# Weight loading of a convolution and feed-forward kernel: the first matrix in four transfers, the second in two buffers shared with the output

## The chip, the cores and the metric

The kernel runs on one core of one Trainium2 chip. The metric is the device time of one execution in microseconds (us). A run that differs by less than 0.2%, some 2.3 us here, is counted as the same.

## The reference

Two stages follow each other. The first is a causal convolution over seven positions whose weights are made for each token and each of eight heads by a softmax; the second is a feed-forward layer of width 2048.

```python
w = exp(weight_gen - max(weight_gen)); w = w / (sum(w) + 1e-09)      # (4, 4096, 8, 7)
x = einsum('bshk,bskhg->bshg', w, x_unf)      # 7 rows of x, ending at the token; 192 columns
h = x.reshape(16384, 192) @ w_in              # 192 x 2048
g = where(h >= 1, h, where(h <= -1, 0, (h + 1) ** 2 / 4))
out = (g @ w_out).astype(float32)             # 2048 x 192
```

The matrices `w_in` and `w_out` arrive as 64-bit floating point numbers, 3.15 MB each; the kernel turns them into 32-bit ones itself.

## The kernel before

The 16384 tokens are worked through in 32 blocks of 512. For one block the 2048 columns of `w_in` are 16 pieces of 128, taken two at a time: eight "pairs" for a block, 256 in all. Each pair has a first product (`gemm1_pair`, 18 matmuls), an activation on ScalarE and VectorE (`relu`, `square`, `act_g`, `split_g`), and a second product (`gemm2_part`, twice 16 matmuls), which is issued two pairs later. The convolution of later blocks runs on GpSimd beside this. All instructions stand on their engine in the order in which the code is written, so an instruction that waits holds up everything behind it on its engine.

The weights are decoded once, in the pairs of the first block, in eight chunks; chunk c is what pair c needs: 192 x 256 numbers of `w_in` ("part 0") and 256 x 192 of `w_out` ("part 1"). For each part `cast_act` (ScalarE) or `cast_dve` (VectorE) makes the upper bits in a buffer `head`, of which there are two; `merge` (VectorE) shifts the lower bits in and writes `psw` in PSUM; `high` (ScalarE) and `low` (VectorE) split the result in two summands, `whi` and `wlo` for part 0, `wo` for part 1. `marks` holds the VectorE steps so that GpSimd's part of the convolution of block 1 (`wave`) goes behind them.

`load_weights(c)` fills a buffer `r` from a pool of four with three transfers on SyncE's queue (SP): one for each half of the partitions from `w_in`, one for 128 partitions from `w_out`. A row of `w_in` in such a transfer has 128 numbers, 1024 bytes. Chunks 0, 1 and 2 are issued first, then the tokens of block 1 (`load_x(1)`), then chunk 3. Chunks 4 to 7 are issued when the buffer of the chunk four places before is free. The first transfer is held back until a step of the softmax of block 0 (`marks[6]`). The store of a finished block goes through a tile `osb` from a pool of two. A transfer also waits for the one issued eight places before it on the same queue.

In the code that sets the beginning in order, the steps stand so:

```python
add(3)
cast_act(0, 0)
again(own[0])
...                       # the transposes of block 0 follow, on TensorE
merge(0, 0)
cast_dve(0, 1)
...
cast_dve(1, 2)            # both parts of chunk 1 in one instruction
merge(1, 0)
```

`again` copies 64 columns of a tile of the convolution, so that the transposes (`turn_sum`, line 267) of block 0 can read it; they wait for the last of these copies.

Of the kernel before, what the change touches and what calls it, by code (L numbers as in the profile page):

```python
# [22 lines left out]
def kernel(  # L23
# [22 lines left out]
    P = 128  # L46
    B, S, D = x.shape
# [6 lines left out]
    Q = P // 2  # L54
    NC = D // Q
# [20 lines left out]
    raw = ctx.enter_context(tc.tile_pool(name="raw", bufs=4))  # L76
# [7 lines left out]
    op = ctx.enter_context(tc.tile_pool(name="op", bufs=2))  # L84
# [10 lines left out]
    heads = [const.tile([P, (D // Q) * P + 2 * D, 2], U16, tag=f"head{m}", name="head") for m in range(2)]  # L95
# [4 lines left out]
    def run(ops):  # L100
        for o in ops:
            o()
# [194 lines left out]
    CF = 2  # L297
    C1 = NC * P
    CN = C1 + CF * D
    NCH = NF // CF  # L300
    UNIT = 2.0 ** 8
    raw_t, marks = {}, []

    def load_weights(c, behind=None):
        r = raw.tile([P, 4 * CN + 2], U16, tag="r", name="r")
        for h in range(2):
            f = c * CF + h
            load = nc.sync.dma_start(
                out=r[h * Q:(h + 1) * Q, 1:1 + 4 * C1].rearrange("q (k c) -> q k c", k=NC),
                in_=w_in[:, f * P:(f + 1) * P].rearrange("(k q) c -> q k c", q=Q).bitcast(U16))  # L310
            if behind is not None:
                tc.add_manual_dep(load.ins, behind.ins.name, SYNC, reason="the first block goes first")
                behind = None
        nc.sync.dma_start(
            out=r[:, 1 + 4 * C1:1 + 4 * CN].rearrange("p (f c) -> p f c", f=CF),
            in_=w_out[c * CF * P:(c + 1) * CF * P, :].rearrange("(f p) c -> p f c", p=P).bitcast(U16))
        raw_t[c] = r

    def tops(c, part):

        sl = (slice(0, C1), slice(C1, CN), slice(0, CN))[part]
        top = raw_t[c][:, 2:2 + 4 * CN].rearrange("p (c t) -> p c t", t=4)[:, sl, 2]
        return heads[c % 2][:, sl, 1].bitcast(F16), top.bitcast(BF16)

    def cast_act(c, part):
        o, i = tops(c, part)
# [2 lines left out]
    def cast_dve(c, part):  # L329
        o, i = tops(c, part)  # L330
        marks.append(nc.vector.tensor_scalar(out=o, in0=i, scalar1=0.5, scalar2=None, op0=ALU.mult))  # L331

    psw = {}

    def merge(c, part):
        word = raw_t[c].bitcast(U32)[:, 1:1 + 2 * CN].rearrange("p (c t) -> p c t", t=2)[:, :, 0]
        upper = heads[c % 2].rearrange("p c t -> p (c t)").bitcast(U32)
        psw[c, part] = ps_h.tile([P, 512], F32, tag="h", name="psw")
        sl = (slice(0, C1), slice(C1, CN))[part]
        marks.append(nc.vector.scalar_tensor_tensor(  # L340
            out=psw[c, part].bitcast(U32)[:, 0:sl.stop - sl.start], in0=word[:, sl], scalar=13, in1=upper[:, sl],
            op0=ALU.logical_shift_right, op1=ALU.bitwise_or))

    def views(c, part):
# [5 lines left out]
    def high(c, part):  # L350
        hi, lo, src = views(c, part)
        nc.scalar.activation(out=hi, in_=src, func=AF.Copy)
# [95 lines left out]
    def evac(b):  # L448

        t0 = b * N  # L450
        osb = op.tile([P, 4, D], F32, tag="osb", name="osb")
        pos = o_t.pop(b)
        by_turn = osb.rearrange("p (k m) d -> p m k d", m=n // 2)
        ops = []
        for m in range(n // 2):
            ops.append(lambda m=m: nc.scalar.activation(out=by_turn[:, m], in_=pos[m][:, :, D:2 * D], func=AF.Copy, scale=UNIT ** 2))  # L456
            ops.append(lambda m=m: nc.vector.scalar_tensor_tensor(  # L457
                out=by_turn[:, m], in0=pos[m][:, :, 0:D], scalar=UNIT ** 2, in1=by_turn[:, m],
                op0=ALU.mult, op1=ALU.add))

        def store(m=None):
            rows = out[t0:t0 + N, :]
            if b < 2:
                nc.sync.dma_start(out=rows.rearrange("(p j) d -> p (j d)", j=n), in_=osb.rearrange("p j d -> p (j d)"))
            elif m is None:
                nc.sync.dma_start(out=rows.rearrange("(a q) d -> q a d", q=P), in_=osb)
            else:
                nc.sync.dma_start(out=rows.rearrange("(k m q) d -> q m k d", q=P, m=n // 2)[:, m], in_=by_turn[:, m])

        return ops, store  # L470
# [60 lines left out]
    with tc.manual_schedule():  # L531
# [10 lines left out]
        clear_x(1)  # L542
        s0, s1 = softmax(0), softmax(1, nc.gpsimd, nc.gpsimd)
        marks += [o() for o in s0[0:3] + s1[0:2] + s0[3:]]
        load_weights(0, marks[6])
        load_weights(1)
        load_weights(2)
        load_x(1)
        load_weights(3)
        run(s1[2:4])  # L550
        alone, near, far, second, add, own = conv_summed(0)
        src = [ps_h.tile([P, 512], F32, tag="h", name="psx") for _ in range(NC)]
# [16 lines left out]
        run(s1[4:6])  # L569
        low(0, 0)  # L570
        run(split_x(0, src, [nc.vector] * NC))
        cast_dve(1, 2)
        merge(1, 0)
        turned1 = whole()
        n_ops = conv(1, nc.gpsimd, marks, turned1)
# [10 lines left out]

        def first_pairs():
            merge(0, 1)
            merge(1, 1)
            tc.add_manual_dep(s1[6]().ins, marks[-1].ins.name, SYNC, reason="the decoding of a chunk goes first")  # L590
            load_weights(4)
            load_weights(5)
            relu(0)
            high(1, 0)
            low(1, 0)
            gemm1_pair(1)
            cast_act(2, 0)
            high(0, 1)
            high(1, 1)
            low(0, 1)  # L600
            low(1, 1)
            cast_dve(2, 1)
            merge(2, 0)
            merge(2, 1)
            wave(3)
            load_weights(6)
            square(0)
            relu(1)
            high(2, 0)
            high(2, 1)  # L610
            square(1)
            act_g(0)
            low(2, 0)
            low(2, 1)
            act_g(1)
            split_g(0)
            relu(2)
            square(2)
            split_g(1)
            relu(3)  # L620
            square(3)
            act_g(2)
            act_g(3)
            split_g(2)
            split_g(3)
            cast_act(3, 0)
            cast_dve(3, 1)

        def early_pair(w):
            i, j, c = 2 * w, 2 * w + 1, w + 1  # L630
            merge(c, 0)
            merge(c, 1)
            wave(1)
            if c + 4 < NCH:
                load_weights(c + 4)
            relu(i)
            high(c, 0)
            high(c, 1)
            low(c, 0)
            low(c, 1)  # L640
            square(i)
            relu(j)
            square(j)
            act_g(i)
            if c + 1 < NCH:
# [28 lines left out]
        for w in range(NS // 2 + LAGP):  # L674
            i, j = 2 * w, 2 * w + 1
# [74 lines left out]
```

## Time and profile before

| | |
|---|---|
| runs | 1160.45, 1161.01, 1163.01 us; median 1161.01 |
| profiled execution, first to last instruction (span) | 1158.6 us, 2.4 us under the median of the runs |
| TensorE busy | 1145.0 us, 99% of the span |
| VectorE, ScalarE, GpSimd busy | 72%, 83%, 68% |
| moved by DMA | 91.43 MB, 79 GB/s in the mean |

The span is the time inside the program; the difference to the runs lies around it. TensorE is PE in the rows, its weight loads PEld; VectorE is DVE, ScalarE is ACT, GpSimd is POOL, SyncE's queue is SPq. A time in a row counts from the start of the span. "Busy" of TensorE includes time in which a matmul waits inside the engine, so 99% alone does not say that it does useful work at its peak.

### The profile page before, as it was taken

The page shows a single profiled execution, that of the slowest core. Times are in us where ns is not written, and L with a number is a line of the kernel's source. Part 1 is how long each engine was busy: PE and PEld are TensorE (multiplying, and loading weights), DVE is VectorE, ACT ScalarE, POOL GpSimd, SP SyncE. Part 2 cuts the span into 40 slices and gives each one's busy share as a digit, 9 for nine tenths or more (in the row PEclk, how much of TensorE's full clock was granted, in tenths as well). Part 3 has the DMA queues.
Part 4 walks back from the last instruction along what each step waited for, and adds up shares of the span by engine and source line. Part 5 has one row for each costly group of instructions (what it writes and reads, how often), then busy time and mean ns, then how long its engine had stood idle before and what let it go on. Part 6 is the DMA issues. An engine that isn't in the chain of part 4 may idle for free.

```text
span 1158.6 us, 32197 instructions
## 1 busy us (share of the span) xinstructions
PE 1145.0 (99%) x12885; PEld 1038.1 (90%) x12885; DVE 834.1 (72%) x1271; ACT 964.7 (83%) x1745; POOL 792.5 (68%) x511
## 2 busy tenths in 40 slices
PE   7999999999999999999999999999999999999998
PEld 5799999999999999999999999999999999999997
DVE  8887767677676776767777676776767767677664
ACT  6878888888888888888888888888888888888886
POOL 4788976667857678486686866678576785866310
PEclk9999999999999999999999999999999999999999
DMA  9422222212222212222121222222222122221100
GB/s 229 112 82 79 77 84 90 89 64 73 75 77 90 84 61 82 71 87 90 56 89 59 85 89 90 64 73 74 76 90 95 51 85 70 80 90 57 47 24 15
DMA packets 84052, 91.43 MB, mean 79 GB/s; under 512 B 5056, under 2 KB 75712, under 8 KB 83904
## 3 DMA queue, kind: packets, MB, share of 16 engines
q1 hardware_dynamic: 83904, 89.39, 24.0%
q8 instruction: 101, 1.65, 0.6%
q14 instruction: 47, 0.39, 0.1%
HBM read 64.99 MB, written 24.38 MB: 77 GB/s over the span
## 4 chain that ended last, share of the span: by engine, by line
PE 95%; ACT 2%; DMA 2%; DVE 1%; issue 0%; POOL 0%; DVEq 0%; POOLq 0%; ACTq 0%; SPq 0%
PE o L432 48%; PE psh L378 45%; DMA r<-in_moe_w_in_dram 1%; PE psx L267 1%; DMA r<-in_moe_w_out_dram 1%; PE psx L208 0%; ACT u L392 0%; DVE psh L397 0%; ACT u L389 0%; ACT gh L403 0%; DVE psw L340 0%; DVE gl L404 0%; POOL piece L189 0%; POOL acc L189 0%; ACT hc L258 0%
## 5 line engine op out<-in xcount | busy, mean ns | idle before, releaser
L432 PE MATMUL o<-wo,gh 64*128 64x384 f32 x4096 | 612.2, 355 | 1.5 <-SPq L441 1.4
L397 DVE SCALAR_TENSOR_TENSOR psh<-u,psh 128x512 f32<-128x512 f32 x512 | 354.7, 696 | 299.6 <-ACT u L392 299.4
L432 PE MATMUL o<-wo,gl 64*128 64x192 f32 x4096 | 542.7, 251 | 0.0
L432 PEld LDWEIGHTS o<-wo,gh 64*128 64x128 f32 x4096 | 421.1, 184 | 13.1 <-SPq L441 2.3
L432 PEld LDWEIGHTS o<-wo,gl 64*128 64x128 f32 x4096 | 421.3, 187 | 9.0
L389 ACT ACTIVATE u<-psh 128x512 f32<-128x512 f32 x512 | 301.5, 589 | 93.2 <-PE psh L378 91.2
L404 DVE TENSOR_TENSOR gl<-psh,gh 128x512 fp32r<-128x512 f32 x512 | 345.7, 686 | 15.3 <-ACT gh L403 1.1
L403 ACT ACTIVATE gh<-psh 128x512 fp32r<-128x512 f32 x512 | 299.2, 592 | 65.5 <-DVE psh L397 65.5
L378 PE MATMUL psh<-hc,whi 64*128 64x512 f32 x1536 | 349.8, 404 | 3.7 <-DVE wlo L356 1.9
L189 POOL TENSOR_TENSOR acc<-acc,pr 128x768 f32<-128x768 f32 x185 | 343.8, 1858 | 5.7 <-DVE head L331 2.0
L378 PE MATMUL psh<-hl,whi 64*128 64x512 f32 x1536 | 337.7, 391 | 0.0
L378 PE MATMUL psh<-hc,wlo 64*128 64x512 f32 x1536 | 337.3, 390 | 0.0
L392 ACT ACTIVATE u<-u 128x512 f32<-128x512 f32 x512 | 323.7, 632 | 16.0
L179 POOL TENSOR_TENSOR pr<-x,w 128x768 f32<-128x768 f32 x186 | 286.8, 1549 | 7.1 <-DVE psw L340 7.1
L259 POOL TENSOR_TENSOR hl<-XT,hc 128x512 fp32r<-128x512 f32 x90 | 115.4, 1297 | 221.2 <-ACT hc L258 221.2
L378 PEld LDWEIGHTS psh<-hl,whi 64*128 64x128 f32 x1536 | 173.6, 185 | 34.7 <-DVE hl L259 0.3
L378 PEld LDWEIGHTS psh<-hc,whi 64*128 64x128 f32 x1536 | 173.0, 185 | 29.4 <-DVE wlo L356 4.3
L378 PEld LDWEIGHTS psh<-hc,wlo 64*128 64x128 f32 x1536 | 174.1, 187 | 21.4
L179 POOL TENSOR_TENSOR acc<-x,w 128x768 f32<-128x768 f32 x31 | 47.9, 1547 | 72.5 <-DVE w L155 70.6
L258 ACT ACTIVATE hc<-XT 128x512 fp32r<-128x512 f32 x90 | 55.5, 618 | 0.0
L284 DVE STREAM_TRANSPOSE T<-acc 128x768 f32<-128x768 f32 x30 | 50.9, 1698 | 0.3 <-POOL acc L189 0.3
L457 DVE SCALAR_TENSOR_TENSOR osb<-o,osb 128x384 f32<-128x384 f32 x64 | 32.7, 556 | 2.7 <-ACT osb L456 2.7
(44 smaller groups left out, 188.8 us busy)
## 6 DMA issues: line engine op xcount, KB each, us to landing
x<-in_x_dram SPq DMA_DIRECT2D x28, 960.0 KB
XT<-D SPq DMA_DIRECT2D x180, 128.0 KB
out_dram<-osb SPq DMA_DIRECT2D x31, 384.0 KB
D<-T SPq DMA_DIRECT2D x30, 384.0 KB
x<-in_x_dram SPq DMA_DIRECT2D x4, 945.0 KB
w<-in_weight_gen_dram SPq DMA_DIRECT2D x15, 224.0 KB
r<-in_moe_w_in_dram SPq DMA_DIRECT2D x16, 192.0 KB
r<-in_moe_w_out_dram SPq DMA_DIRECT2D x8, 384.0 KB
```

Of the source, the lines that this page charges most:

```text
L179: held(eng.tensor_tensor(out=t, in0=xtile[:, k:k + n, :].rearrange("p j (h g) -> p j h g", h=H), in1=wt[:, gi, :, :, k:k + 1].to_broadcast ...
L189: held(eng.tensor_tensor(out=o, in0=s, in1=t, op=ALU.add))
L258: ops.append(lambda c=c: nc.scalar.activation(out=hc[:, c], in_=src[c], func=AF.Copy))
L259: ops.append(lambda c=c: lows.append(engines[c].tensor_tensor(out=hl[:, c], in0=src[c], in1=hc[:, c].bitcast(F32), op=ALU.subtract)))
L284: lambda: nc.vector.transpose(out=T.rearrange("p b c j -> p b j c"), in_=acc.rearrange("p j (r b) -> p b j r", b=R)),
L378: nc.tensor.matmul(out=pair[h][:, 0:N], lhsT=l[rows, f // 2, (c + h) % NC if b < 2 else c], rhs=r[rows, c], start=(s == 0), stop=(s == len ...
L389: nc.scalar.activation(out=u_t[i], in_=h_t[i][:, 0:N], func=AF.Relu, scale=0.5 * UNIT, bias=0.5)
L392: nc.scalar.activation(out=u_t[i], in_=u_t[i], func=AF.Square, scale=UNIT ** -0.5)
L397: nc.vector.scalar_tensor_tensor(out=pv, in0=uv, scalar=1.0 / UNIT, in1=pv, op0=ALU.min, op1=ALU.max)
L403: nc.scalar.activation(out=gh[:, 0:N], in_=gv, func=AF.Copy)
L404: nc.vector.tensor_tensor(out=gl[:, 0:N], in0=gv, in1=gh[:, 0:N].bitcast(F32), op=ALU.subtract)
L432: mm = nc.tensor.matmul(out=o_t[b][turn][:, k, 0:cols], lhsT=g_t[i][l][rows, t * P:(t + 1) * P], rhs=wo[rows, f].rearrange("p s d -> p (s ...
```

## The change

`w_in` is loaded by `load_in` for four chunks at once: two calls, each with two transfers (one for each half of the partitions), 192 rows of 512 numbers, 4096 bytes, each. So that these columns are neighbours, chunk c now has the columns c and 8 + c (in pieces of 128) instead of 2c and 2c + 1, and `load_out` takes the rows of `w_out` to match. `load_out(c)` still loads 256 rows of `w_out`, 1536 bytes to a row, in one transfer over 128 partitions, but into one of the two tiles `osb`, which the stores use later. `cast_dve(1, 2)` becomes two instructions, and `cast` and `merge` read part 0 in three pieces of 128 columns.

```diff
-    def load_weights(c, behind=None):
-        r = raw.tile([P, 4 * CN + 2], U16, tag="r", name="r")
+    def load_in(c, behind=None):
+        r = raw.tile([P, 4 * WIDE * C1 + 2], U16, tag="ri", name="ri", bufs=2)
         for h in range(2):
-            f = c * CF + h
+            at = (h * NCH + c) * P
             load = nc.sync.dma_start(
-                out=r[h * Q:(h + 1) * Q, 1:1 + 4 * C1].rearrange("q (k c) -> q k c", k=NC),
-                in_=w_in[:, f * P:(f + 1) * P].rearrange("(k q) c -> q k c", q=Q).bitcast(U16))
+                out=r[h * Q:(h + 1) * Q, 1:1 + 4 * WIDE * C1].rearrange("q (k c) -> q k c", k=NC),
+                in_=w_in[:, at:at + WIDE * P].rearrange("(k q) c -> q k c", q=Q).bitcast(U16))
...
+    def load_out(c):
+        r = op.tile([P, 4 * CF * D + 2], U16, tag="osb", name="ro")
         nc.sync.dma_start(
-            out=r[:, 1 + 4 * C1:1 + 4 * CN].rearrange("p (f c) -> p f c", f=CF),
-            in_=w_out[c * CF * P:(c + 1) * CF * P, :].rearrange("(f p) c -> p f c", p=P).bitcast(U16))
-        raw_t[c] = r
+            out=r[:, 1:1 + 4 * CF * D].rearrange("p (f c) -> p f c", f=CF),
+            in_=w_out.rearrange("(h s p) c -> s p h c", h=2, p=P)[c].bitcast(U16))
+        out_t[c] = r
...
-        load_weights(0, marks[6])
-        load_weights(1)
-        load_weights(2)
+        load_in(0, marks[6])
+        load_out(0)
+        load_out(1)
         load_x(1)
-        load_weights(3)
+        load_in(4)
...
-        cast_dve(1, 2)
+        cast_dve(1, 0)
+        cast_dve(1, 1)
         merge(1, 0)
...
             merge(0, 1)
             merge(1, 1)
...
-            load_weights(4)
-            load_weights(5)
+            load_out(2)
+            load_out(3)
...
-            load_weights(6)
+            load_out(4)
...
-            if c + 4 < NCH:
-                load_weights(c + 4)
+            if c + 2 < NCH:
+                load_out(c + 2)
```

Two places show how the order on the engines changes. The first is SyncE's queue at the beginning, from the first weight transfer on; `r` is the buffer of a chunk, `DMAHW` with a number is a wait for an earlier transfer, `DVE`, `PE` and `Activation` are waits for those engines. Before:

```order
L308 DMA r<-in_moe_w_in_dram 64x3x512 [waits DVE_49]
L308 DMA r<-in_moe_w_in_dram 64x3x512
L314 DMA r<-in_moe_w_out_dram 128x2x768
L308 DMA r<-in_moe_w_in_dram 64x3x512 [waits DMAHW0_49]
L308 DMA r<-in_moe_w_in_dram 64x3x512 [waits DMAHW1_49]
L314 DMA r<-in_moe_w_out_dram 128x2x768 [waits DMAHW2_49]
L308 DMA r<-in_moe_w_in_dram 64x3x512 [waits DMAHW3_49]
L308 DMA r<-in_moe_w_in_dram 64x3x512 [waits DMAHW4_49]
L314 DMA r<-in_moe_w_out_dram 128x2x768 [waits DMAHW5_49]
L126 DMA x<-in_x_dram 128x1920 [waits DMAHW6_49]
```

And the same place of the change, where `ri` is the buffer of `w_in` for four chunks and `ro` that of `w_out` for one:

```order
L309 DMA ri<-in_moe_w_in_dram 64x3x2048 [waits DVE_49]
L309 DMA ri<-in_moe_w_in_dram 64x3x2048
L320 DMA ro<-in_moe_w_out_dram 128x2x768
L320 DMA ro<-in_moe_w_out_dram 128x2x768 [waits DMAHW0_49]
L126 DMA x<-in_x_dram 128x1920 [waits DMAHW1_49]
L309 DMA ri<-in_moe_w_in_dram 64x3x2048 [waits DMAHW2_49]
L309 DMA ri<-in_moe_w_in_dram 64x3x2048 [waits DMAHW3_49]
L320 DMA ro<-in_moe_w_out_dram 128x2x768 [waits DMAHW7_49,DMAHW4_49,DVE_49]
L320 DMA ro<-in_moe_w_out_dram 128x2x768 [waits DMAHW5_49,DMAHW0_49,DVE_49]
```

The transfer of `w_out` for chunk 2 stood ahead of the tokens of block 1; now it stands behind them and behind both transfers of `w_in` for chunks 4 to 7, and it waits for VectorE besides.

The second place is VectorE, from the cast of chunk 1 to the activation of the first pair (`psw`, `whi`, `wlo`, `wo` and `head` as above). Before:

```order
L331 TENSOR_SCALAR head<-r 128x768 [waits DMAHW2_49,DMAHW1_49,DMAHW0_49]
L340 SCALAR_TENSOR_TENSOR psw<-r,head 128x384 [waits DVE_49]
L340 SCALAR_TENSOR_TENSOR psw<-r,head 128x384 x2
L356 TENSOR_TENSOR wlo<-psw,whi 128x384 [waits Activation_49]
L356 TENSOR_TENSOR wo<-psw,wo 128x2x192 [waits Activation_49] x2
L331 TENSOR_SCALAR head<-r 128x384 [waits DMAHW5_49]
L340 SCALAR_TENSOR_TENSOR psw<-r,head 128x384 [waits DMAHW4_49,DMAHW3_49,DVE_49]
```

And of the change:

```order
L347 TENSOR_SCALAR head<-ri 128x384
L347 TENSOR_SCALAR head<-ro 128x384 [waits DMAHW0_49]
L356 SCALAR_TENSOR_TENSOR psw<-ri,head 128x384 [waits DVE_49]
L356 SCALAR_TENSOR_TENSOR psw<-ro,head 128x384
L356 SCALAR_TENSOR_TENSOR psw<-ro,head 128x384 [waits DVE_49]
L373 TENSOR_TENSOR wlo<-psw,whi 128x384 [waits Activation_49]
L373 TENSOR_TENSOR wo<-psw,wo 128x2x192 [waits Activation_49] x2
L347 TENSOR_SCALAR head<-ro 128x384 [waits DMAHW4_49,DVE_49]
```

The order of the steps is the same but for the cast that became two. The last row is the cast of chunk 2's `w_out`; the transfer that it waits for is the one that the second merge in these rows lets go.

## Rows read from the trace of the kernel before

**Rows 1.** Page, part 1: busy time, share of the span, instructions.

```profile
PE 1145.0 (99%) x12885; PEld 1038.1 (90%) x12885; DVE 834.1 (72%) x1271; ACT 964.7 (83%) x1745; POOL 792.5 (68%) x511
```

**Rows 2.** Chain that ended last, 0 to 110 us: start, length, what.

```profile
20.21 11.32 DMA r<-in_moe_w_in_dram
...
31.55 6.98 DMA r<-in_moe_w_out_dram
...
56.86 0.66 PE psx L267 x4
...
58.84 2.12 PE psh L378 x18
60.95 2.27 PE o L432 x32
```

**Rows 3.** Busy time by stretch: stretch, length, engines, PEclk, DMA share, GB/s.

```profile
24.00:30.00 6.00, 4.09 (x44) 3.39 (x42) 5.36 (x11) 5.21 (x11) 2.94 (x3) 1.00 1.10 199
...
sum 42.00, PE 36.77 PEld 29.10 DVE 39.14 ACT 35.38 POOL 22.93; mean PE 5.25 PEld 4.16 DVE 5.59 ACT 5.05 POOL 3.27
```

**Rows 4.** Waits of the engines, 0 to 60 us: all that name a DMA.

```profile
POOL piece L227 <- DMA x<-in_x_dram: 1.2, 1, 1.2
...
DVE m L149 <- DMA w<-in_weight_gen_dram: 0.8, 2, 0.4
```

**Rows 5.** Timeline of ACT and POOL: start, length, what, [idle before <- releaser].

```profile
6.92 4.54 POOL L227 TENSOR_TENSOR piece<-x,w 128x768 f32<-128x768 f32 x3 [1.18 <-DMA x<-in_x_dram]
...
11.81 0.63 ACT L327 ACTIVATE head<-r 128x384 f16<-128x384 bf16 x1
12.64 0.42 ACT L169 ACTIVATE piece<-piece 128x256 f32<-128x256 f32 x1 [0.19 <-DVE piece L244]
```

**Rows 6.** Timeline of DVE, 12 to 39 us.

```profile
12.99 0.38 DVE L331 TENSOR_SCALAR head<-r 128x384 f16<-128x384 bf16 x1
...
16.46 0.61 DVE L331 TENSOR_SCALAR head<-r 128x768 f16<-128x768 bf16 x1
17.10 1.50 DVE L340 SCALAR_TENSOR_TENSOR psw<-r,head 128x384 uint32<-128x384 uint32 x3
...
20.14 0.39 DVE L331 TENSOR_SCALAR head<-r 128x384 f16<-128x384 bf16 x1
...
24.64 0.69 DVE L404 TENSOR_TENSOR gl<-psh,gh 128x512 fp32r<-128x512 f32 x1 [0.48 <-ACT gh L403]
...
28.07 1.03 DVE L340 SCALAR_TENSOR_TENSOR psw<-r,head 128x384 uint32<-128x384 uint32 x2
...
36.01 0.39 DVE L331 TENSOR_SCALAR head<-r 128x384 f16<-128x384 bf16 x1
...
37.16 1.45 DVE L404 TENSOR_TENSOR gl<-psh,gh 128x512 fp32r<-128x512 f32 x2
```

**Rows 7.** Timeline of SyncE's queue: when transfers are issued.

```profile
5.80 1.36 SPq L308 DMA_DIRECT2D r<-in_moe_w_in_dram  x2
...
11.75 0.47 SPq L126 DMA_DIRECT2D x<-in_x_dram  x1
```

**Rows 8.** DMA view, 0 to 8 us: GB/s in 40 slices of 0.2 us.

```profile
GB/s 0 0 0 0 0 0 0 0 22 148 246 215 224 237 305 502 234 86 499 307 307 499 230 384 384 307 307 461 346 269 85 0 0 0 0 0 51 138 236 318
```

**Rows 9.** DMA views of 11:12, 27:28, 13:14 and 17:19.5 us, in this order.

```profile
DMA packets 181, 0.17 MB, mean 173 GB/s; under 512 B 12, under 2 KB 181, under 8 KB 181
...
DMA packets 191, 0.18 MB, mean 184 GB/s; under 512 B 15, under 2 KB 191, under 8 KB 191
...
DMA packets 210, 0.30 MB, mean 296 GB/s; under 512 B 8, under 2 KB 210, under 8 KB 210
...
DMA packets 223, 1.06 MB, mean 422 GB/s; under 512 B 16, under 2 KB 103, under 8 KB 223
```

**Rows 10.** Timeline of PE, 19 to 29 us: pair 1's end, pair 2's start.

```profile
20.86 0.61 PE L378 MATMUL psh<-hl,whi 64*128 64x512 f32 x2
22.56 0.96 PE L378 MATMUL psh<-hc,whi 64*128 64x512 f32 x2 [1.08 <-DVE wlo L356]
```

More of the change, by code (lines that the diff above doesn't have):

```diff
@@ L301 @@
     UNIT = 2.0 ** 8
-    raw_t, marks = {}, []
-    def load_weights(c, behind=None):
-        r = raw.tile([P, 4 * CN + 2], U16, tag="r", name="r")
+    WIDE = 4
+    in_t, out_t, marks = {}, {}, []
+    def load_in(c, behind=None):
+        r = raw.tile([P, 4 * WIDE * C1 + 2], U16, tag="ri", name="ri", bufs=2)
         for h in range(2):
-            f = c * CF + h
+            at = (h * NCH + c) * P
             load = nc.sync.dma_start(
-                out=r[h * Q:(h + 1) * Q, 1:1 + 4 * C1].rearrange("q (k c) -> q k c", k=NC),
-                in_=w_in[:, f * P:(f + 1) * P].rearrange("(k q) c -> q k c", q=Q).bitcast(U16))
+                out=r[h * Q:(h + 1) * Q, 1:1 + 4 * WIDE * C1].rearrange("q (k c) -> q k c", k=NC),
+                in_=w_in[:, at:at + WIDE * P].rearrange("(k q) c -> q k c", q=Q).bitcast(U16))
             if behind is not None:
@@ L313, in load_weights, with raw_of, head_of @@
                 behind = None
+        for k in range(WIDE):
+            in_t[c + k] = r
+    def load_out(c):
+        r = op.tile([P, 4 * CF * D + 2], U16, tag="osb", name="ro")
         nc.sync.dma_start(
-            out=r[:, 1 + 4 * C1:1 + 4 * CN].rearrange("p (f c) -> p f c", f=CF),
-            in_=w_out[c * CF * P:(c + 1) * CF * P, :].rearrange("(f p) c -> p f c", p=P).bitcast(U16))
-        raw_t[c] = r
+            out=r[:, 1:1 + 4 * CF * D].rearrange("p (f c) -> p f c", f=CF),
+            in_=w_out.rearrange("(h s p) c -> s p h c", h=2, p=P)[c].bitcast(U16))
+        out_t[c] = r
+    def raw_of(c, part):
+        r = (out_t if part else in_t)[c]
+        k, n_ = (CF, D) if part else (NC, WIDE * P)
+        lo, n1 = (0, D) if part else (c % WIDE * P, P)
+        return r, k, n_, slice(lo, lo + n1)
+    def head_of(c, part):
+        k, n1 = (CF, D) if part else (NC, P)
+        return heads[c % 2][:, (slice(0, C1), slice(C1, CN))[part]].rearrange("p (k c) t -> p k c t", k=k)
     def tops(c, part):
-        sl = (slice(0, C1), slice(C1, CN), slice(0, CN))[part]
-        top = raw_t[c][:, 2:2 + 4 * CN].rearrange("p (c t) -> p c t", t=4)[:, sl, 2]
-        return heads[c % 2][:, sl, 1].bitcast(F16), top.bitcast(BF16)
+        r, k, n_, cols = raw_of(c, part)
+        top = r[:, 2:2 + 4 * k * n_].rearrange("p (k c t) -> p k c t", k=k, t=4)[:, :, cols, 2]
+        return head_of(c, part)[:, :, :, 1].bitcast(F16), top.bitcast(BF16)
     def cast_act(c, part):
@@ L335, in merge @@
     def merge(c, part):
-        word = raw_t[c].bitcast(U32)[:, 1:1 + 2 * CN].rearrange("p (c t) -> p c t", t=2)[:, :, 0]
-        upper = heads[c % 2].rearrange("p c t -> p (c t)").bitcast(U32)
+        r, k, n_, cols = raw_of(c, part)
+        word = r.bitcast(U32)[:, 1:1 + 2 * k * n_].rearrange("p (k c t) -> p k c t", k=k, t=2)[:, :, cols, 0]
+        upper = heads[c % 2].rearrange("p c t -> p (c t)").bitcast(U32)[:, (slice(0, C1), slice(C1, CN))[part]]
         psw[c, part] = ps_h.tile([P, 512], F32, tag="h", name="psw")
-        sl = (slice(0, C1), slice(C1, CN))[part]
         marks.append(nc.vector.scalar_tensor_tensor(
-            out=psw[c, part].bitcast(U32)[:, 0:sl.stop - sl.start], in0=word[:, sl], scalar=13, in1=upper[:, sl],
+            out=psw[c, part].bitcast(U32)[:, 0:C1].rearrange("p (k c) -> p k c", k=k), in0=word, scalar=13,
+            in1=upper.rearrange("p (k c) -> p k c", k=k),
             op0=ALU.logical_shift_right, op1=ALU.bitwise_or))
@@ L450, in evac @@
         t0 = b * N
-        osb = op.tile([P, 4, D], F32, tag="osb", name="osb")
+        osb = op.tile([P, 4 * D + 1], F32, tag="osb", name="osb")[:, 0:4 * D].rearrange("p (j d) -> p j d", j=4)
         pos = o_t.pop(b)
```

## The prediction

> **What bounds the kernel now.** I read the busy times first: TensorE is busy for 1145.0 of 1158.6 us [rows 1]. Since such a time holds waits too, I then read the chain that ended last. From 56.86 us on it is matmuls and nearly nothing else, in pairs of 2.12 + 2.27 = 4.4 us [rows 2]; whatever moves that point moves the end by as much, since TensorE has no idle time behind it to make it up. So the change is worth what it does to the first 57 us, in which all its transfers lie.
>
> What bounds that part? The chain puts 11.32 + 6.98 = 18.3 us of it down to the weights' transfers [rows 2]. I don't take this at its word. VectorE is busy 39.14 of the 42 us from 12 to 54 us [rows 3], and among the waits of the computing engines only two name a DMA, for the tokens and for the weights of the softmax, before 7 us [rows 4]. At 38.5 us, where the chain changes over from a DMA to VectorE, VectorE had just ended a subtraction that ran from 37.16 for 1.45 us [rows 6]: the data had been there before it was free. So the decoding, in turns on VectorE and ScalarE, sets the pace, and the transfers come in time. The reader is to see that an earlier transfer is worth next to nothing here, and a later one costs in full once it passes the moment at which VectorE or ScalarE asks for it.
>
> **When the transfers land before.** The first weight transfer is issued at 5.80 us [rows 7]; its data begins to flow in the slice from 7.2 us, after a pause since about 6.2, when the tokens of block 0 were through [rows 8]. GpSimd could use those tokens at 6.92 [rows 5], so 0.7 us pass from the last data to its use. Transfers of the queue run in the order of issue: the tokens of block 1, issued at 11.75, are the long rows that the stretch 17 to 19.5 us holds (120 packets above 2 KB), 5 us later [rows 7, 9].
>
> How fast do they run? From 11 to 12 and from 27 to 28 us, 0.17 MB in 181 packets and 0.18 MB in 191 are rows of 1024 bytes of `w_in`, and the rate is 173 and 184 GB/s. From 13 to 14 us, 0.30 MB in 210 packets are for the most part rows of 1536 bytes of `w_out`: 296 GB/s. The stretch with the rows of 7680 bytes has 422 GB/s [rows 9]. Over 16 engines, 1024 bytes at 173 GB/s are 95 ns to a row, and 1536 bytes at 296 GB/s are 83 ns. The longer row takes less time, so the length of a row is not what makes `w_in` slow. What else differs is that a transfer of `w_in` writes 64 partitions, the others 126 or 128. The change makes the rows four times as long and keeps the 64 partitions.
>
> So the unknown price is the rate of 4096-byte rows into 64 partitions. Bounds: 173 GB/s, if length does nothing, and 422 GB/s, if length does all. Half the rate of the transfers over all partitions would be 211. I take 200, near the lower rows, since the partitions are what separates them. The Trainium skill, "SBUF — State Buffer", section "Door 1: The DMA port swizzle (why `[64,N]` ≈ `[32,N]`)", says that a transfer into partitions 0 to 63 reaches eight of the sixteen write ports and tends to 218 GB/s. The 173 and 184 GB/s agree with that; by 218 the sum below would be 7.9 instead of 9.3 us.
>
> **The change step by step, at 200 GB/s.** Times on the queue first. The first two transfers of `w_in` are 1.573 MB instead of 0.393 for the same first chunk: 7.9 us from 7.2, to 15.1; usable at 15.8. Then `w_out` of chunks 0 and 1, 0.393 MB each at 296 GB/s = 1.3 us: usable at 17.1 and 18.4. The tokens of block 1, 0.98 MB at 422 GB/s = 2.3 us: the queue is at 20.0. Both transfers of `w_in` for chunks 4 to 7: 7.9 us, to 27.9. Then `w_out` of chunk 2, 1.3 us: to 29.2, usable at 29.9.
>
> - *First delay.* ScalarE's cast of chunk 0 stood at 11.81 [rows 5] and now waits until 15.8: 4.0 us. Behind it on ScalarE stands the last copy (`again`, 12.64), for which the transposes of block 0 wait, and VectorE's first merge waits for the cast too. VectorE's cast of chunk 0's `w_out` stood at 12.99 [rows 6] and now waits until 17.1: 4.1 us. All behind it moves by that.
> - *One cast made two.* 2 x 0.39 instead of 0.61 us [rows 6] = 0.17 us. The casts of chunk 1 move from 16.46 to 20.6 and find their data there (18.4).
> - *Second delay.* The second of the three merges that began at 17.10 [rows 6] now ends at about 22.4 and releases the buffer for chunk 2's `w_out`. An empty queue would deliver it at 22.4 + 1.4 (from issue to first data, as 5.80 to 7.2) + 1.3 + 0.7 = 25.8. But 1.57 MB of `w_in` for chunks that are wanted much later stand ahead, so it comes at 29.9. VectorE's cast of chunk 2 stood at 20.14 [rows 6]: 9.8 us, in which the first delay and the 0.17 us are contained. Behind this cast stand all of VectorE's work and, through merges and products, ScalarE's, TensorE's and GpSimd's.
> - *Given back.* During the stall ScalarE finishes what VectorE waited for at 24.64, 0.48 us [rows 6]. I count 0.5.
> - *The rest of `w_out`.* Chunk 3 follows chunk 2 directly. Chunk 5 is issued once chunk 3 is merged, 28.07 + 1.03 + 9.3 = 38.4, and usable 3.4 us later at 41.8; its cast stands at 36.01 + 9.3 = 45.3 [rows 6]. So two buffers do from there on, with 3.5 us to spare; the other late chunks repeat this. The stores reuse the tiles only after the first block, when all chunks have long been merged.
> - *Reading in three pieces.* No row shows this for a cast or merge. I take nothing; the nearest is the copy of 4 x 64 numbers at 0.42 us [rows 5] against 0.38 for VectorE's cast of 384 in one run [rows 6], so 0.04 us a step at most, below 1 us over the 16 merges and 7 casts. On the other side no gain either: they move as many numbers. 12 transfers less to issue are worth nothing, since SyncE's queue runs ahead.
>
> Sum: 9.8 - 0.5 = 9.3 us. Span 1158.6 + 9.3 = 1167.9; with the 2.4 us around it 1170.3 us.
>
> At 173 GB/s each pair of transfers takes 9.1 us: chunk 2 at 32.3, sum 11.7, 1172.7 us. At 300 GB/s it takes 5.2: the queue ahead is empty at 22.6, chunk 2 usable at 24.6; sum 4.0, 1165.0.
>
> **The rivals.**
> 1. *Length does all* (422 GB/s). A pair of transfers takes 3.7 us: chunk 0 is usable at 11.6, before ScalarE asks; chunk 2 is released at about 18.3 and usable 3.4 us later, 21.7, against 20.14. 1.6 - 0.5 = 1 us: 1162 us, the same within measurement. For it speaks the length of the rows at 422; against it, that 1536-byte rows already beat 1024-byte ones in time to a row.
> 2. *Faster.* The chain is right and transfers do hold back chunks 3 to 5. Then the early `w_in` takes waits away, and chunk 2 must come by 20.14, which is the point that decides. What could be won is at most VectorE's idle time, 42 - 39.14 = 2.9 us: 1158.1. Against it speak the waits [rows 4] and chunk 2's later release.
> 3. *TensorE's clock falls in the stall.* It is 1.00, 2.4 GHz, in the stretches of rows 3, and the longest gap of these pairs is about 1.1 us [rows 10]. Now pair 1 ends at 21.5 + 4.3 = 25.8 and pair 2 starts at 22.56 + 9.8 = 32.4: 6.6 us idle. A pair at 1.2 GHz would take 4.4 us longer, of which I give ScalarE's lead at least 2 back: about 2 us on top, 1172.5. The Trainium skill, "TensorE: Matmul & The Clock Gate", section "HAM oscillation — how this bites in real kernels", says that such waits let the clock fall; no stretch here shows it.
>
> **Chances.** 1168 to 1172 by the sum: 0.60. Clock or 173 GB/s, 1172 to 1174: 0.13. A rate between, 1164 to 1168: 0.13. Rival 1, the same: 0.09. Rival 2: 0.05. The measurement can tell a difference of about 0.2%, 2.3 us, from none. Slower is then 0.86, same 0.09, faster 0.05. The range 1164 to 1174 us leaves out 0.14; the likeliest case's own is 1168 to 1172.
>
> **What would show it.** Right: ScalarE idle before the first cast of `head` until about 15.8 us, VectorE idle before chunk 2's cast until about 30, both put down to DMA; 170 to 220 GB/s in stretches with `w_in` alone; the pair of 4.4 us beginning at about 66 instead of 57 us, and no difference in the pairs after that. Wrong: stretches of `w_in` at 300 GB/s or more, or chunk 2's transfer not held up by those ahead of it; then the delays shrink as worked out. A granted clock below 1.00 between 26 and 45 us would be rival 3.

## The result and the profile after

The changed kernel takes 1177.62 us (median of four runs, 1177.15 to 1178.16), the kernel before 1161.47 us (median of four, 1160.45 to 1163.01). The ratio is 1.0141, interval 1.0129 to 1.0153: slower by 16.2 us, where 9.3 were forecast. The profiled execution has a span of 1175.4 us, 16.8 more than before.

**The start.** The chain that ended last, 0 to 110 us, of the changed kernel (start, length, what):

```profile
6.55 10.27 DMA ri<-in_moe_w_in_dram
...
22.99 8.51 DMA ro<-in_moe_w_out_dram
...
68.32 0.66 PE psx L267 x4
...
70.30 2.10 PE psh L395 x18
72.40 2.27 PE o L449 x32
```

The steady pairs begin at 68.32 instead of 56.86 us [rows 2]: 11.46 us later, and the two transfers that hold the chain are those of the forecast. Before, the chain named transfers too, though no computing engine was ever idle for one of the weights; now engines do wait for them. ScalarE's timeline, with the idle time before an instruction and its releaser in brackets:

```profile
16.90 0.63 ACT L343 ACTIVATE head<-ri 128x384 f16<-128x384 bf16 x1 [4.72 <-DMA ri<-in_moe_w_in_dram]
```

and VectorE's:

```profile
17.56 0.57 DVE L356 SCALAR_TENSOR_TENSOR psw<-ri,head 128x384 uint32<-128x384 uint32 x1 [4.90 <-ACT head L343]
...
31.59 0.38 DVE L347 TENSOR_SCALAR head<-ro 128x384 f16<-128x384 bf16 x1 [5.17 <-DMA ro<-in_moe_w_out_dram]
...
36.09 0.69 DVE L421 TENSOR_TENSOR gl<-psh,gh 128x512 fp32r<-128x512 f32 x1 [0.48 <-ACT gh L420]
```

ScalarE's first cast moved from 11.81 [rows 5] to 16.90, VectorE's cast of chunk 2 from 20.14 [rows 6] to 31.59. Around these two waits TensorE stood still twice, and its clock fell. Busy time by stretch (PE, PEld, DVE, ACT, POOL, then the granted clock, the DMA share and GB/s):

```profile
18.00:24.00 6.00, 5.27 (x22) 3.30 (x22) 5.39 (x13) 2.42 (x5) 0.43 (x1) 0.50 1.04 283
...
30.00:36.00 6.00, 1.99 (x9) 1.53 (x11) 4.02 (x8) 3.51 (x8) 2.97 (x2) 0.57 0.35 119
36.00:42.00 6.00, 5.31 (x48) 4.36 (x46) 5.75 (x11) 5.21 (x11) 2.93 (x3) 0.86 0.06 4
```

The timeline of TensorE shows what stood ahead of each fall:

```profile
17.84 1.12 PE L267 MATMUL psx<-ident,piece 128*128 128x128 f32 x4 [3.36 <-ACT piece L169]
...
34.01 1.26 PE L395 MATMUL psh<-hc,whi 64*128 64x512 f32 x2 [6.50 <-DVE wlo L373]
```

After 3.36 us of idle time the granted clock is 0.50, the lower of its two levels, and after 6.50 us it is so again: the row from 30 to 36 us shows 0.57 for the whole stretch, and its last two us, in which TensorE works again, show 0.50.

**The transfers.** The DMA views of 13:14 and 22:24 us, both with 4096-byte rows of `w_in`:

```profile
DMA packets 47, 0.19 MB, mean 193 GB/s; under 512 B 0, under 2 KB 0, under 8 KB 47
...
DMA packets 96, 0.36 MB, mean 182 GB/s; under 512 B 7, under 2 KB 7, under 8 KB 96
```

Rows of 1024 bytes had 173 and 184 GB/s [rows 9]. Four times the length brought next to nothing. The next view is of the same kernel from 16.8 to 17.8 us, with the rows of `w_out`, 1536 bytes each, into 128 partitions:

```profile
DMA packets 259, 0.40 MB, mean 396 GB/s; under 512 B 13, under 2 KB 256, under 8 KB 259
```

Rows of less than half the length go twice as fast. One short stretch does not fit: from 8.4 to 9.2 us 64 packets of 4096 bytes of `w_in` went at 328 GB/s. The transfers for both halves of the partitions had been issued by then; whether they ran beside each other there, no view shows, and it stays open.

**Behind the start.** The forecast had no difference here, and there are three: a gain in each pair, a wait in each block, and a wait at the very end. The end of the chain before:

```profile
1131.68 2.12 PE psh L378 x18
...
1144.84 2.12 PE psh L378 x18
1146.95 6.66 PE o L432 x92
```

and after:

```profile
1146.46 2.10 PE psh L395 x18
...
1159.56 2.10 PE psh L395 x18
1161.66 6.66 PE o L449 x92
...
1169.45 1.92 DMA out_dram<-osb
...
1171.48 0.50 ACT osb L473
```

Three pairs take 1144.84 - 1131.68 = 13.16 us before and 1159.56 - 1146.46 = 13.10 after: 4.387 and 4.367 us for one, the difference lying in the 18 matmuls of the first product (2.12 and 2.10). Over 256 pairs that would *win* the change 5.1 us; the run below that moves nothing but the tiles measures 4.6. At the very end it loses: the second copy into `osb`, ScalarE's of the second half, now waits for the store of the first half. From the last matmul to the end of the span were 1158.6 - 1153.61 = 5.0 us and are 1175.4 - 1168.32 = 7.1: 2.1 us lost. And in each block something waits for `osb`; the groups of the page for its copy, its sum and the weight load behind them (busy, mean ns, idle before and releaser):

```profile
L449 PEld LDWEIGHTS o<-wo,gh 64*128 64x128 f32 x4096 | 389.6, 184 | 18.3 <-DVE osb L474 6.8
...
L473 ACT ACTIVATE osb<-o 128x384 f32<-128x384 f32 x64 | 30.9, 484 | 34.8 <-DVE osb L474 29.3
...
L474 DVE SCALAR_TENSOR_TENSOR osb<-o,osb 128x384 f32<-128x384 f32 x64 | 35.5, 555 | 24.4 <-ACT osb L473 24.4
```

The view of the tile `osb` before names no such thing (who sat idle before its instructions, for how many us and times):

```profile
PE o L432: 2.9, 1
ACT osb L456: 2.7, 1
```

The order of the instructions tells why. Before, on ScalarE, the two halves of a block's evacuation:

```
L456 ACTIVATE osb<-o_407 128x2x192 [waits PE_49]
L456 ACTIVATE osb<-o_408 128x2x192 [waits PE_49]
```

and after:

```
L473 ACTIVATE osb<-o_396 128x2x192 [waits DMAHW6_49,DMAHW4_49,DMAHW7_49,DMAHW0_49,PE_49]
L473 ACTIVATE osb<-o_397 128x2x192 [waits DVE_49,PE_49]
```

One line of the diff, not quoted ahead of the prediction, makes the tile one 32-bit number longer, so that it is as large as `ro`, and cuts the result out of it:

```diff
-        osb = op.tile([P, 4, D], F32, tag="osb", name="osb")
+        osb = op.tile([P, 4 * D + 1], F32, tag="osb", name="osb")[:, 0:4 * D].rearrange("p (j d) -> p j d", j=4)
```

The first half writes the rows 0 and 2 of this view, the second the rows 1 and 3. Before, the second half's copy waited for TensorE alone; now it also waits until VectorE is through with the first half, though the two share no number.

**The sum of the difference.** Start 11.46, weight loads of the next block behind `osb` 6.8, first product -5.1, tail 2.1: 15.3 of 16.8 us. The last product begins at 1161.66 instead of 1146.95, 14.71 us later, of which 11.46 + 6.8 - 5.1 = 13.2 are named; the other 1.5 us come up again in the experiment with the cut tile alone, below.

### The profile page after: what moved, and what is told of

It is laid out like the page before. It is cut to its first block, busy times and chain, and to the rows that moved or that the text cites. A ratio compares the mean times of both kernels' runs of the same rounds, so it can differ in the third digit from the quotient of the medians.

```text
span 1175.4 us, 32149 instructions
## 1 busy us (share of the span) xinstructions
PE 1149.8 (98%) x12885; PEld 1033.9 (88%) x12885; DVE 838.3 (71%) x1272; ACT 965.5 (82%) x1745; POOL 793.2 (67%) x511
## 4 chain that ended last, share of the span: by engine, by line
PE 86%; DVE 5%; ACT 5%; DMA 2%; issue 1%; POOL 0%; SPq 0%; DVEq 0%; ACTq 0%; POOLq 0%
PE o L449 45%; PE psh L395 41%; ACT u L409 2%; DVE psh L414 1%; ACT u L406 1%; DMA ri<-in_moe_w_in_dram 1%; ACT gh L420 1%; DVE gl L421 1%; DVE T L284 1%; DMA ro<-in_moe_w_out_dram 1%; DVE osb L474 1%; DVE psw L356 0%; ACT osb L473 0%; DMA w<-in_weight_gen_dram 0%; DVE w L155 0%
## 5 line engine op out<-in xcount | busy, mean ns | idle before, releaser
L449 PE MATMUL o<-wo,gl 64*128 64x192 f32 x4096 | 516.9, 247 | 0.0
L449 PEld LDWEIGHTS o<-wo,gh 64*128 64x128 f32 x4096 | 389.6, 184 | 18.3 <-DVE osb L474 6.8
L449 PEld LDWEIGHTS o<-wo,gl 64*128 64x128 f32 x4096 | 395.2, 187 | 10.5
L395 PE MATMUL psh<-hc,whi 64*128 64x512 f32 x1536 | 320.8, 400 | 10.6 <-DVE wlo L373 7.2
L395 PE MATMUL psh<-hl,whi 64*128 64x512 f32 x1536 | 313.0, 393 | 0.0
L395 PE MATMUL psh<-hc,wlo 64*128 64x512 f32 x1536 | 310.7, 389 | 0.0
L395 PEld LDWEIGHTS psh<-hc,whi 64*128 64x128 f32 x1536 | 151.6, 185 | 37.7 <-DVE wlo L373 9.7
L395 PEld LDWEIGHTS psh<-hl,whi 64*128 64x128 f32 x1536 | 151.3, 185 | 32.9 <-DVE hl L259 0.3
L395 PEld LDWEIGHTS psh<-hc,wlo 64*128 64x128 f32 x1536 | 152.1, 187 | 23.3
L473 ACT ACTIVATE osb<-o 128x384 f32<-128x384 f32 x64 | 30.9, 484 | 34.8 <-DVE osb L474 29.3
```

The lines of the kernel that those rows point to most:

```text
L395: nc.tensor.matmul(out=pair[h][:, 0:N], lhsT=l[rows, f // 2, (c + h) % NC if b < 2 else c], rhs=r[rows, c], start=(s == 0), stop=(s == len ...
L449: mm = nc.tensor.matmul(out=o_t[b][turn][:, k, 0:cols], lhsT=g_t[i][l][rows, t * P:(t + 1) * P], rhs=wo[rows, f].rearrange("p s d -> p (s ...
```

## The experiments

Four questions were open: what the cut of `osb` costs, what makes the matmuls faster, what the start consists of (row length, partitions, queue order), and what the clock costs.

**The halves of a store made to lie apart.** The second product's blocks of rows are dealt out so that each half fills two neighbouring rows of `osb`.

```diff
-                t = turn + k * n // 2
+                t = turn * (n // 2) + k
...
-        by_turn = osb.rearrange("p (k m) d -> p m k d", m=n // 2)
+        by_turn = osb.rearrange("p (m k) d -> p m k d", m=n // 2)
```

> The change with one part set right: the two halves of a stored block lie one behind the other in the tile osb (the group of 128 tokens is turn*2+k instead of turn+2*k, in the second product and in the store alike), so that the range that the first half writes no longer overlaps the range of the second. Theory (two causes: 11.5 us at the start from late weight transfers, 5.3 us later from a wait between the two halves of each block's evacuation, about 1.6 us in the middle at 30 blocks, 1.9 around the first blocks and 2.1 at the end): the start stays, the rest goes, 1172.3 us; ScalarE's second copy of a block waits for no VectorE instruction. Rival (the rest comes from the tile's odd size of 3076 bytes, or from the later clock): 1177.6 us as the change.

Measured: 1166.97 us against 1160.79, ratio 1.0053 (1.0038 to 1.0068); 10.65 us less than the change, or 10.0 us when each is set against the kernel before as measured beside it (16.15 and 6.18 us). The waits are gone; the tile's view:

```profile
PE o L449: 2.9, 1
ACT osb L473: 2.7, 1
```

The steady pairs begin at 68.32 as in the change, so the gain lies wholly behind the start. The kind was right and the size twice what was expected, because the faster first product had hidden as much: only without the waits did its 5 us show.

**The cut alone, in the kernel before.** The one line of the diff above and nothing else.

> The kernel before with one part of the change alone: osb is a tile of 769 numbers of which the first 768 are sliced and viewed as four rows; the loading is as before. Theory (the slice makes the second half of each evacuation wait for the first): 1161.5 + 5.3 = 1166.8 us, the pairs start at 57 us as before. Rival (the later loss needs the shared buffers or the late start): 1161.5 us.

Measured: 1171.52 us, ratio 1.0091 (1.0076 to 1.0106), 10.7 us over the kernel before, with its slower pairs. The tile's view:

```profile
DVE osb L457: 29.3, 31
ACT osb L456: 24.5, 33
```

The waits are those of the change. The page puts 6.0 us of TensorE's weight loads down to them, and the tail ends with a store as above. Its last product begins at 1154.76, 7.8 us later than before: 1.8 more than those 6.0, much like the remainder that the sum above left open. Of the 1.8 us 0.23 are a later start (57.09 against 56.86). Where the rest lies is argued from the chain and no run separates it: about the end of the second block VectorE's work is on the path itself, and the chain of the change has there:

```profile
115.07 0.47 DVE osb L474
...
115.62 0.49 ACT osb L473
```

In the kernel before no instruction of `osb` is on the chain at that place. One line, which copies no number more, costs two thirds of what the whole change lost.

**The transfers for chunks 4 to 7 moved behind `w_out` of chunks 2 and 3.**

```diff
         load_x(1)
-        load_in(4)
...
             load_out(2)
             load_out(3)
+            load_in(4)
```

> The change with one line moved: the two transfers of w_in for chunks 4 to 7 are issued behind w_out of chunks 2 and 3 instead of ahead of them. Theory (chunk 2's w_out stands in the queue behind 1.57 MB that nobody needs yet): VectorE's cast of chunk 2 begins at 26.4 instead of 31.6 us, which is when VectorE itself gets there; 1172.4 us. What is left of the start is the first delay, 5.1 us, and about 1.1 us of a slow clock. Rival (chunk 2's transfer is late for its own release and way): the cast stays near 31 us, 1177.6 us.

Measured: 1172.83 us, ratio 1.0106 (1.0089 to 1.0123). VectorE's cast of chunk 2 no longer waits:

```profile
27.07 0.39 DVE L347 TENSOR_SCALAR head<-ro 128x384 f16<-128x384 bf16 x1
```

In this profiled execution the weights of the softmax came later and everything with them (first cast 17.79 instead of 16.90), so 27.07 - 0.89 = 26.2 is to be set against 31.59: the place in the queue alone cost this cast about 5.4 us, and the run 4.8.

**All 128 partitions.** One transfer into all 128 partitions, of other rows of `w_in`, in place of two transfers into 64 each.

```diff
-        for h in range(2):
-            at = (h * NCH + c) * P
+        for h in range(1):
             load = nc.sync.dma_start(
-                out=r[h * Q:(h + 1) * Q, 1:1 + 4 * WIDE * C1].rearrange("q (k c) -> q k c", k=NC),
-                in_=w_in[:, at:at + WIDE * P].rearrange("(k q) c -> q k c", q=Q).bitcast(U16))
+                out=r[:, 1:1 + 4 * WIDE * C1].rearrange("q (k c) -> q k c", k=NC),
+                in_=w_in[0:P, 0:NC * WIDE * P].rearrange("q (k c) -> q k c", k=NC).bitcast(U16))
```

> The change with each pair of half transfers of w_in replaced by one transfer of as many bytes and rows of 4096 bytes over all 128 partitions; it takes the rows 0 to 127 of w_in with 1536 columns each, so the first product uses other weights than the reference's. Theory (64 partitions set the rate, not the length of a row): 1.57 MB take 4 us instead of 8.5, stretches with w_in alone show 360 GB/s or more, ScalarE's cast of chunk 0 waits less than 1 us, VectorE's cast of chunk 2 begins at 22 to 23 us; 1168 to 1169 us with the later wait unchanged. Rival (the pitch of 16 KB between rows of w_in in memory, or the destination two bytes off an even address, sets the rate): 180 to 190 GB/s as now, 1177.6 us.

Measured: 1169.25 us, ratio 1.007 (1.0055 to 1.0085). ScalarE's cast of chunk 0 waits no more, and VectorE's of chunk 2 begins at 22.70, both as expected. The stretch in which this transfer runs and the next ones begin, and the DMA view of 9 to 10 us, in which it runs alone:

```profile
9.00:12.00 3.00, 2.89 (x26) 2.89 (x27) 2.97 (x5) 1.25 (x3) 3.00 (x3) 1.00 0.96 391
```

```profile
DMA packets 36, 0.44 MB, mean 442 GB/s; under 512 B 0, under 2 KB 0, under 8 KB 0
```

The last row shows that the edit did more than its text says. 0.44 MB in 36 packets are 12288 bytes each, not 4096: the 1536 columns of a row lie side by side in memory and in the buffer, so a row goes as one piece. The partitions were doubled and the length of a row was tripled, and this run alone doesn't separate the two. The rivals named ahead of it lose weight: the rows still begin 16 KB apart in memory and two bytes off in the buffer, and the rate is twice that of 64 partitions all the same. Against the length speak the rows of `w_out` above: 1536 bytes at 396 GB/s over 128 partitions, 4096 bytes at 182 to 193 over 64. That the partitions set the rate fits all these rows but the short stretch at 328 GB/s; it is argued from them together, not shown by one run, since none has rows of 4096 bytes over 128 partitions. The steady pairs begin at 59.45 us in its chain, 2.6 later than before: most of the start's loss goes with the rate, even with the change's order on the queue.

**TensorE kept busy.** To price the clock, seven idle matmuls of 128 x 512 were put ahead of the last transposes, on top of the moved transfers.

```diff
+            if k == len(pieces) - 1:
+                drive(7, ps_o.tile([P, 2, 512], F32, tag="o0", name="idle")[:, 0])
```

> The kernel with w_in for chunks 4 to 7 issued later, and seven idle matmuls more ahead of the last transposes of block 0, so that TensorE does not stand still while ScalarE waits for chunk 0. Theory (part of the late start is TensorE's clock, which shows 0.50 to 0.72 in the stretches after the standstill): pair 0 takes 2.5 instead of 4.2 us, VectorE's first low part of chunk 1 waits about 1 us less for ScalarE, and all of the start moves forward by about 1.1 us: 1171.5 against 1172.8 us. Rival (the clock costs nothing because VectorE waits for data anyway): 1172.8 us.

Measured: 1172.42 us, ratio 1.0099 (1.0084 to 1.0114), no difference to 1172.83. Its timeline tells that it could not answer:

```profile
13.56 1.67 PE L208 MATMUL idle<-ident 128*128 128x512 bf16 x7
...
18.13 0.65 PE L267 MATMUL psx<-ident,piece 128*128 128x128 f32 x4 [2.02 <-ACT piece L169]
```

The seven ran at once and were done at 15.2; TensorE still stood 2.02 us, and from 21 to 24 us it was granted 0.62. Inconclusive.

**Two chunks to a transfer.** Half the first transfer (2048-byte rows), three tiles `ro`, and the halves of a store lying apart. `w_in` of chunks 6 and 7 is issued behind `w_out` of chunk 3.

```diff
-    WIDE = 4
+    WIDE = 2
...
         load_out(1)
+        load_in(2)
+        load_out(2)
         load_x(1)
         load_in(4)
...
-            load_out(2)
             load_out(3)
+            load_in(6)
+            load_out(4)
```

> The change with the two halves of a stored block apart, and with w_in for two chunks to a transfer instead of four (rows of 2048 bytes, three buffers), w_out and the stores in three buffers instead of two, and w_in of chunks 2 and 3 and w_out of chunk 2 issued ahead of the tokens of block 1. Theory (what costs at the start is how much must land before chunk 0 and chunk 2, not the kind of transfer): chunk 0 usable at 12.2 to 12.6 us, the start later than before by 0.5 to 1 us; with the first product at 2.10 instead of 2.12 us as in the other kernels of the change, 1156 to 1157 us. If that pace hangs on something that this kernel does not share with them, 1161 to 1162.

Measured: 1165.86 us, ratio 1.0041 (1.0026 to 1.0056). Missed: chunks 0 to 2 came nearly in time, and the wait moved one chunk on.

```profile
31.65 0.38 DVE L347 TENSOR_SCALAR head<-ro 128x384 f16<-128x384 bf16 x1 [2.66 <-DMA ro<-in_moe_w_out_dram]
35.94 0.39 DVE L347 TENSOR_SCALAR head<-ro 128x384 f16<-128x384 bf16 x1 [1.22 <-DMA ro<-in_moe_w_out_dram]
```

`w_out` of chunk 3 stood behind `w_in` of chunks 4 and 5, and `w_out` of chunk 4 behind `w_in` of chunks 4 to 7, the order of the change again; the steady pairs begin at 61.78, 4.9 us late. No run moves these transfers, so that the order makes this wait is argued from the run before. The pairs were also slower than in the change, 2.12 us for the first product; this loading puts the tiles elsewhere (`hc` at 0, counted as below), which led to the next runs.

**Where the tiles lie.** Four buffers `r` of 6148 bytes, each rounded up to 6176, are 24704 bytes; two `ri` of 12292, rounded to 12320, are 24640. So all that lies behind them begins 64 bytes lower in the change: `hc` and `hl`, from which the first product reads its tokens, at 480 instead of 32 counted within 512 bytes, by the program's own allocation. The weights `whi`, `wlo` and `wo` lie at the same place in all kernels. Nothing else in the instructions of a steady pair differs. An unused tile ahead of the buffers moves them in the kernel before without any other edit:

```diff
+    raw.tile([P, 112], F32, tag="pad", name="pad", bufs=1)
```

With 448 bytes (`hc` at 480, as in the change):

> The kernel before with nothing changed but an unused tile of 448 bytes ahead of the weight buffers, so that all tiles behind them lie at the same place within 512 bytes as in the change (480, before 32). Theory (the change's first product is faster, 2.097 instead of 2.116 us for 18 matmuls, because of where its operands lie): 2.097 us here too, 256 pairs times 0.019 = 5 us less: 1156 us. Rival (the pace comes from the other mapping of columns to chunks or from anything else in the change): 1160.8 us.

Measured: 1156.29 us against 1160.86, ratio 0.9961 (0.9947 to 0.9976): 4.6 us less, where 5 were expected. Its chain near the end:

```profile
1138.22 2.27 PE o L433 x32
1140.49 2.10 PE psh L379 x18
```

With 64 bytes (`P, 16`; `hc` at 96):

> As the kernel with 448 bytes, but with 64: the tiles behind lie at 96 within 512 bytes. If every place but the old one is good, 1156 us; if the place within 512 bytes matters and 480 is a good one, anything from 1156 to 1161 us, and the time of 18 matmuls says which.

Measured: 1159.71 us, ratio 0.9993 (0.9983 to 1.0003), the same as before. Here the second product is the faster one:

```profile
1142.04 2.26 PE o L433 x32
1144.29 2.12 PE psh L379 x18
```

The first run reproduces the change's 2.10 us with the old loading. The reverse, the change with 64 unused bytes ahead of its buffers:

> The change with 64 unused bytes ahead of the weights' buffers, so that hc lies at 32 within 512 bytes as in the kernel before; nothing else moves on any engine. Theory, that the change's faster first product (2.097 instead of 2.116 us) is due to the place of its tiles alone: 2.116 again, 5.1 us slower than the change, 1182.7 us. Rival, that the new order of the columns or the loading makes the pace: 2.097 and 1177.6 us.

Measured: 1181.87 us, ratio 1.0171 (1.0156 to 1.0186), 4.25 us over the change, where 5.1 were expected; its pairs begin at 67.87 instead of 68.32, which accounts for 0.45 of the rest.

```profile
69.85 2.12 PE psh L396 x18
71.97 2.27 PE o L450 x32
```

So the place of the tiles alone makes the faster matmuls; loading and column order have no part in it. Last, both pads in the kernel before, the second ahead of `gh` and `gl`, which the second product loads as its weights (the rows `LDWEIGHTS o<-wo,gh`; `wo` is what it streams):

```diff
+    raw.tile([P, 112], F32, tag="pad", name="pad", bufs=1)
+    gp.tile([P, 32], F32, tag="pad2", name="pad2", bufs=1)
```

> The kernel before, with the unused 448 bytes ahead of the weights' buffers (hc at 480 within 512 bytes, which gave 2.097 us for the 18 matmuls of the first product and 1156.3 us) and 128 unused bytes ahead of gh and gl (at 96, where the second product took 2.264 instead of 2.274 us). Theory, that each product follows the place of its own tokens' operand: 2.097 + 2.264 us, 256 x 0.01 = 2.6 us less, 1153.7 us. Rival, that one place for all tiles matters or that the first product's gain is lost when the two differ: 1156 to 1160 us.

Measured: 1153.20 us against 1161.52, ratio 0.9923 (0.9906 to 0.9939), the fastest of all kernels here.

```profile
1135.64 2.25 PE o L434 x32
1137.89 2.10 PE psh L380 x18
```

The second product gained when its own tiles moved; the first kept its gain.

**Both remedies in the change.** The halves apart, and the late transfers behind.

> The change with both remedies: the halves of a store that don't overlap (alone 1166.97) and w_in for chunks 4 to 7 issued behind w_out of chunks 2 and 3 (alone 4.8 us better than the change). Theory, that the two losses lie in different stretches and add up: 1166.97 - 4.8 = 1162.2 us, within 0.2% of before. Rival, that the earlier start is used up by the first blocks' evacuations or a later wait: 1165 to 1167 us.

Measured: 1161.79 us against 1161.52, ratio 1.0002 (0.9993 to 1.0011). The losses add up as expected. VectorE's casts for chunks 1 and 2, and between them its last step of chunk 1:

```profile
20.94 0.58 DVE L347 TENSOR_SCALAR head<-ri 128x384 f16<-128x384 bf16 x1
...
25.13 1.02 DVE L373 TENSOR_TENSOR wo<-psw,wo 128x384 fp32r<-128x384 f32 x2 [0.29 <-ACT wo L369]
26.07 0.39 DVE L347 TENSOR_SCALAR head<-ro 128x384 f16<-128x384 bf16 x1
```

From the cast of chunk 1 to that step are 25.13 - 20.94 = 4.19 us; before they were 19.20 - 16.46 = 2.74 [rows 6]. The row of 19.20 in the kernel before, and the cast and the step in the run over 128 partitions, whose engines have the same steps in the same order:

```profile
19.20 1.02 DVE L356 TENSOR_TENSOR wo<-psw,wo 128x384 fp32r<-128x384 f32 x2
```

```profile
17.47 0.58 DVE L346 TENSOR_SCALAR head<-ri 128x384 f16<-128x384 bf16 x1
...
20.21 1.02 DVE L372 TENSOR_TENSOR wo<-psw,wo 128x384 fp32r<-128x384 f32 x2
```

There it is 20.21 - 17.47 = 2.74 us again. What differs is TensorE's clock while it works on pair 0, for which ScalarE and then VectorE wait. The first of the next rows is of the run over 128 partitions, in which TensorE did not stand still ahead of pair 0, the second of the run with both remedies, in which it stood for 3.28 us.

```profile
15.00:18.00 3.00, 3.00 (x27) 2.17 (x24) 2.94 (x7) 1.58 (x3) 0.00 (x0) 1.00 1.03 434
```

```profile
18.00:24.00 6.00, 4.99 (x22) 3.00 (x20) 5.13 (x12) 2.59 (x6) 0.69 (x1) 0.51 0.36 141
```

So the lower clock costs 4.19 - 2.74 = 1.45 us here, and making one cast two costs nothing at that place.

In its chain the steady pairs begin at 62.86 instead of 56.86 us: the loading that is left, with the fall of the clock, still costs the start 6.0 us; the faster first product, some 5 us, pays most of it back. The change's idea has no gain of its own: the kernel before with the same place of tiles is at 1156.29.

## Why the prediction was wrong

The direction was right, and the start went nearly as worked out; the size was not, since two effects behind the start, 10.7 us lost and some 5 won, were not in the sum. The start alone would have made some 1161.5 + 11.5 = 1173 us.

- *The stores.* The step that failed: "The stores reuse the tiles only after the first block, when all chunks have long been merged", by which `osb` was counted at nothing. That is true of the transfers, but the edit of the tile's shape was not looked at. The waits of ScalarE's two copies stood in the order of the changed kernel, to be read without a chip. Alone they cost 10.7 us; of the 10.4 us of span, 6.0 are in weight loads of the next block, 2.6 between the last matmul and the end, and 1.8 are left, which the chain puts for the most part at the second block.
- *No difference behind 57 us.* "Whatever moves that point moves the end by as much, since TensorE has no idle time behind it to make it up." TensorE has none, but its matmuls need not keep their duration. The place of their operands made them 20 ns a pair faster: 5.1 us by the rows, 4.6 with the tiles moved alone. Without the waits the start's 11.46 us end as 5.5 us of span (1164.1 against 1158.6); 0.9 us of that difference have no row of their own.
- *The rate.* 200 GB/s was taken, with 173 as the bound; 182 to 193 were measured in the stretches above, and less at first: 137 from 7.2 to 8.4 us. With the prediction's 0.7 us from landing to use the first pair of transfers took 16.90 - 0.7 - 7.2 = 9.0 us, 175 GB/s in the mean. So the first cast came at 16.90 instead of 15.8 and chunk 2's at 31.59 instead of 29.9. By the prediction's own working at 173 GB/s the sum was 11.7; that 11.46 came so near is in part luck, since the 0.5 us that it takes off were not given back. The mechanism fits what was measured, though no run separates it fully: four times the length did next to nothing at 64 partitions, and the run over 128 had twice the rate, with longer rows as well. The Trainium skill, "SBUF — State Buffer", "Door 1: The DMA port swizzle (why `[64,N]` ≈ `[32,N]`)", also lists 196 GB/s for a transfer of 1 MiB into 64 partitions; that agrees better with these transfers of 0.79 MB than the 218 that the prediction drew from it.
- *The second delay.* Right: chunk 2's `w_out` waited for transfers that nobody wanted yet. With them moved behind it, its cast came 5.4 us sooner and the run was 4.8 us shorter.
- *Given back, 0.5.* It was not: the wait of 0.48 us for `gh` is still there, at 36.09 us. What ScalarE had to do for it stood behind `high` of chunk 2, and that waited 5.70 us, until 32.46, for VectorE's merge; so both engines were moved together.
- *One cast made two, reading in pieces.* From the first of the two casts to the merge behind them were 17.10 - 16.46 = 0.64 us [rows 6]; now 0.72 (21.21 to 21.93). 0.08 instead of 0.17, and a merge still takes 0.57 us. Small, as said.
- *The rest of `w_out`.* Right: no later cast waits for it.
- *Rival 3, the clock.* It fell, to 0.50, already before pair 0 and again before pair 2. In the change the first fall cost nothing, since chunk 2's transfer was later still; the second shows in 36 to 42 us (0.86), but pair 2 began 11.45 us late (34.01 against 22.56 [rows 10]) and the steady pairs 11.46, so nothing was lost between them. With the transfers moved it has a price. It is the 1.45 us of the rows with both remedies above, by which VectorE came later to chunk 2; the run over 128 partitions, at full clock, doesn't have them.

## What to carry to other kernels

Read each edited line for what it does to waits, a tile's shape too: a tile that is cut and viewed may make halves depend on each other that share nothing (here 10 to 10.7 us), and the order of the instructions shows that without a chip. Bytes that are wanted late, issued ahead of bytes that are wanted now on the same queue, can cost much of their transfer time (here 5.4 us for 1.57 MB), and rows of 4096 instead of 1024 bytes did not speed up transfers that reach only half of the partitions. Before a small difference in steady matmuls is put down to an edit, see whether the edit moved their operands, and try an unused tile ahead of them.

## What was not expected of the hardware

The same matmuls on the same numbers take different times by the place of the operand that holds the tokens. The first product streams it (`hc`, `hl`), the second loads it as weights (`gh`, `gl`). The first product's 18 matmuls took 2.12 us with `hc` at 0, 32 or 96 within 512 bytes and 2.10 us at 480; the second product's 32 took 2.27 us with `gh` and `gl` at 0, 32 or 480 and 2.26 and 2.25 us at 96. That is 1% of a product or less, and with both 8.3 us of this kernel (1161.52 against 1153.20). Which of the operands' distances or places decides, and why, no run here shows; only the places named were tried.
